# Blockwise attention into a routed MoE on one core: a transpose target moved to another PSUM bank, ten more empty transposes, and the page's index add moved from GpSimd to VectorE

## The chip, the cores and the metric

The kernel is one program on one core of a Trainium2 chip. Its time is the device time of one launch in microseconds (us). Several launches are timed and their median is compared; one further launch is taken with the hardware profiler, and the rows below come from that one.

The five engines run their own instruction lists and meet at semaphores: TensorE (PE, with its weight loads as PEld), VectorE (DVE), ScalarE (ACT), GpSimd (POOL) and SyncE (SP), which here only starts transfers.

## The reference, cut to what matters

```python
# attention: 8 batches x 8 heads, 576 tokens, head width 64, causal in blocks of 64
scores = q @ k.T / 8, masked where block(row) < block(column)
x = softmax(scores) @ v                      # becomes 4608 tokens x 512
# mixture of experts: 8 experts, one per token
expert = argmax(x @ w_gate);  gate = softmax(x @ w_gate)[expert]
for e in range(8):                           # tokens sorted by expert
    y[e's tokens] = relu(x[e's tokens] @ w1[e]) @ w2[e]     # 512 -> 1024 -> 512
out = gate * y, every token's row put back in its place
```

## The kernel before, in words

**Attention.** The 64 heads are taken two at a time, as 32 pairs. For a pair `p`, `load` fetches q and k, `cast` makes fp16 of them in `h16`, and `trans` turns nine 128x128 blocks on TensorE into a PSUM tile, from which VectorE or ScalarE copies them to `qkT`. `scores_0`, `scores_1` and `scores_2` are the matmuls of the scores into the PSUM tiles `sA` and `sB`, each followed by its exponentials on ScalarE into `pt`; `scores_2` also makes two 64-column pieces (`last_64`), one in `o1[:, 384:448]` and one in `f0[:, 0:64]`, whose exponentials go to `p4`. `attend` multiplies by v into `oP` and `o1`, `sums` and `totals` make the softmax's denominators.

All engines run under a manual schedule: the order in which the Python code is called is the order on each engine. The loop over `p` scores pair `p + 1` while pair `p` is attended. Ahead of the loop stands an **opening** that does the first pair and half of the second: 42 empty transposes (`warm`, which turn the identity and whose result nobody reads), the cast and turns of pair 0, eight more empty turns, the cast of pair 1, `scores_0(0)`, `scores_1(0)`, the turns of pair 1, `scores_2(0)`, and twelve more empty turns. The PSUM tiles are banks of 2 KB per partition: `sA` and `sB` take two each, `oP`, `o1`, `f0` and `f1` one each; `oP16`, `o116`, `f016` and `f116` are the same banks read as fp16.

**MoE.** Tokens are scattered into DRAM in order of expert (`xsorted`), and taken back as pages of 128 rows. This draw has 38 pages, T = 0 to 37. `page(T)` issues, in this order: on TensorE `m1(T)` (32 matmuls into `sA` or `sB`), the four turns of `mtx(T + 2)`, and `m2(T - 1)` (8 matmuls into `oP` or `f0`); on VectorE the copy of page `T + 2`'s first weights into a stage (`mstage`, L614) and the copy of its turned rows (L623); on ScalarE the relu of `m1` (L635) and the scaled copy of `m2`'s result into a buffer y (L647). Then GpSimd makes the token index of page `T - 1` in one of four small tiles (`tos`) by adding a void flag to the index that came with the page (L649, L655; a plain copy at L652), and `write_out` starts the indirect DMA that puts y's rows into `out` (L660). From page 14 on GpSimd also starts the indirect DMA that fetches page `T + 6` (`mload`, L595), behind that page's write. After the fetches of pages 26 and 35, GpSimd is drained (L688). The last pages, from 36, stand in nested conditions, since the number of pages is known only on the chip; the very last write takes `y_last` and `to_last`.

Of the kernel before, what the change touches and what calls it, by code (L numbers as in the profile page):

```python
# [12 lines left out]
ALU = mybir.AluOpType  # L13
# [11 lines left out]
def kernel(  # L25
# [10 lines left out]
    nc = tc.nc  # L36
# [31 lines left out]
    oP16, o116, f016, f116 = (t.bitcast(F16) for t in (oP, o1, f0, f1))  # L68
    sA16 = sA.rearrange("p h f -> p (h f)").bitcast(F16)
    sB16 = sB.rearrange("p h f -> p (h f)").bitcast(F16)  # L70
# [37 lines left out]
    def constants():  # L108
        nc.gpsimd.memset(wg, 0.0)
        nc.gpsimd.memset(picks, 0.0)  # L110
        nc.gpsimd.memset(picks[:, 2 * E + 1:2 * E + 2], 1.0)
        for t in oTs:
            nc.gpsimd.memset(t[:, 576:640], 0.0)

        for t in vts:
            nc.gpsimd.memset(t[0:64, 4], 0.0)
# [37 lines left out]
    def unmixed(did, kind, others):  # L154

        tc.declare_no_dep(did.ins, group=others, reason="the first pages are of other experts")
        tc.add_to_no_dep_group(kind, did.ins)
# [44 lines left out]
    def copy(engine, dst, src):  # L202
        if engine is nc.scalar:
            nc.scalar.activation(dst, src, AF.Copy)  # L204
        else:
            engine.tensor_copy(dst, src)  # L206
# [6 lines left out]
    def warm(ps, n):  # L213

        for _ in range(n):
            nc.tensor.transpose(ps[:, 0:128], ident16, ident16)  # L216

    def trans(p, parts):
        for ps, c0, c1, *engines in parts:
            for c in range(c0, c1):  # L220
                nc.tensor.transpose(ps[:, (c - c0) * 128:(c - c0) * 128 + 128], h16[:, c],  # L221
                                    ident16)
        for n in range(2):
            for ps, c0, c1, *engines in parts:
                to = qkTs[p % 2][:, n].rearrange("d (a p c) -> d a p c", c=9, p=32)
                turned = ps[:, 0:(c1 - c0) * 128].rearrange("d (c a n p) -> d n a p c", n=2,
                                                            a=2, p=32)
                copy(engines[n], to[:, :, :, c0:c1], turned[:, n])
# [15 lines left out]
    def scores_1(p):  # L244
        pt = pts[p % 2]
        score(p, 1, sB, 0, 192, 384)
        score(p, 3, sB, 384, 448, 128)
        exp(pt[:, :, 640:1024], sB[:, :, 0:384])
        exp(pt[:, :, 1088:1216], sB[:, :, 384:512])
# [3 lines left out]
    def scores_2(p):  # L253

        pt, qkT = pts[p % 2], qkTs[p % 2]
        for at, c in enumerate((0, 1, 3, 2)):
            score(p, c, sA, at * 64, c * 128, 64)
        score(p, 2, sA, 256, 320, 256)
        for h, ps in enumerate(last_64):
            r = slice(h * 64, h * 64 + 64)  # L260
            nc.tensor.matmul(out=ps, lhsT=qkT[r, 1, 448:576],
                             rhs=qkT[r, 0, 512:576], start=True, stop=True,
                             skip_group_check=True)
        for h, ps in enumerate(last_64):
            exp(p4s[p % 2][:, h], ps)
        for a, b, w, o in ((0, 1152, 576, 0), (1024, 1408, 192, 128)):
            exp(pt[:, :, a:b].rearrange("p h (c x) -> p h c x", x=w)[:, :, :, 0:64],
                sA[:, :, o:o + 128].rearrange("p h (c x) -> p h c x", c=2), bias=maskb)
        exp(pt[:, :, 1280:1536], sA[:, :, 256:512])
# [103 lines left out]
    def choose(b):  # L373

        lg, mx, val, m2 = (tmp(n, w) for n, w in (
            ("lg", (128, 5, E)), ("mx", 5), ("val", (128, 5, E)), ("m2", 5)))
        oh = ohs[b % 2]
        nc.vector.reduce_max(out=mx, in_=lg, axis=AX.X)
        nc.vector.tensor_tensor(out=lg, in0=lg, in1=over_e(mx), op=ALU.subtract)
        nc.vector.scalar_tensor_tensor(out=val, in0=lg, scalar=0.0, in1=pref,  # L380
                                       op0=ALU.is_equal, op1=ALU.mult)
        nc.vector.reduce_max(out=m2, in_=val, axis=AX.X)
        nc.vector.tensor_tensor(out=oh, in0=val, in1=over_e(m2), op=ALU.is_equal)
# [38 lines left out]
    def scatter(b, j):  # L422
# [14 lines left out]
    rest_e, rest_r, void = (vts[2].rearrange("p c h d -> p (c h d)").bitcast(I32)[  # L437
        :, 512 + i * REST:512 + i * REST + REST] for i in range(3))
# [9 lines left out]
    def spare(i, n):  # L448
# [5 lines left out]
    first_e, first_r, early_void = (  # L454
        ends_of.bitcast(I32)[:, 3 * REST + i * FIRST:3 * REST + i * FIRST + n]
        for i, n in enumerate((FIRST, FIRST, EARLY)))
# [180 lines left out]
    def m2(T, last=False):  # L637
        yp, hT, xs = yps[T % 2], hTs[T % 2], xss[T % XS]
        y, to = (y_last, to_last) if last else (ys[T % len(ys)], tos[T % 4])
        for f in range(8):  # L640
            did = nc.tensor.matmul(  # L641
                out=yp, lhsT=hT[:, f * 128:f * 128 + 128],
                rhs=wall[:, ds(pg[ET.PE, T], 1), 8 + f, :].rearrange("p a f -> p (a f)"),
                start=(f == 0), stop=(f == 7))
            if T < EARLY:
                unmixed(did, "early pages", "late weights")
        nc.scalar.activation(y, yp, AF.Copy, scale=xs.bitcast(F32)[:, 256:257])  # L647
        if T < EARLY:
            nc.gpsimd.tensor_tensor(out=to, in0=xs[:, 257:258], in1=early_void[:, T:T + 1],  # L649
                                    op=ALU.add)  # L650
        elif T < FIRST:
            nc.gpsimd.tensor_copy(to, xs[:, 257:258])  # L652
        else:
            t = T - FIRST
            nc.gpsimd.tensor_tensor(out=to, in0=xs[:, 257:258], in1=void[:, t:t + 1], op=ALU.add)  # L655
        if not last:
            write_out(to, y)

    def write_out(to, y):
        did = nc.gpsimd.indirect_dma_start(  # L660
            out=out[:, :], out_offset=bass.IndirectOffsetOnAxis(ap=to, axis=0),
            in_=y, in_offset=None, bounds_check=N - 1, oob_is_err=False)
        apart("out", did)

    def page(T, first_product=True):

        certain, near = N // 128, 3
        if T + near >= certain + XS - 2 and T + near < PAGES:
            mload(T + near)
        if first_product:  # L670
            m1(T)
        steps = [lambda: m2(T - 1)] if T > 0 else []

        for t in (4, 5) if T == 2 else (T + 3,) if T != 1 else ():
            if t < PAGES:
                mexpert(t, ET.PE)
        if T + 2 < PAGES:
            mexpert(T + 2, ET.DVE)
            mstage(T + 2)

            steps.insert(1 if T == 1 else 0, lambda: mtx(T + 2, xps[T % 2]))
        for step in steps:
            step()
        if 1 < T < certain and T - 2 + XS < certain + XS - 2:
            mload(T - 2 + XS)
        if T in (FIRST, certain - 7):

            nc.gpsimd.drain()  # L688
# [14 lines left out]
    with tc.manual_schedule(engines={ET.PE, ET.Activation, ET.DVE, ET.Pool, ET.SP}):  # L703
# [12 lines left out]
        nc.gpsimd.memset(maskb[0:64], 0.0)  # L716
        scores_0(0)
        scores_1(0)
        trans(1, ((f016, 0, 6, nc.vector, nc.vector), (oP16, 6, 9, nc.vector, nc.vector)))
        scores_2(0)  # L720
        warm(sB16, 12)
        constants()
        load(3)
        cast(2)
        for h in range(2):
            nc.sync.dma_start(
                out=wg[h * 64:h * 64 + 64, :, h * E:h * E + E],
# [152 lines left out]
```

## Time and profile before

| | us |
|---|---|
| median of three runs | 367.33 |
| the three runs | 367.33, 364.81, 367.8 |
| the profiled execution, its own time | 367.39 |
| its span, first to last instruction | 365.5 |
| TensorE busy in the span | 348.9 (95%) |
| GpSimd busy in the span | 241.0 (66%) |

The span is the part of the device time that the trace covers; 1.89 us of the profiled execution lie around it. Busy time counts what an engine executes, and a share of the span is an average over stages that differ. The granted clock of TensorE is a share of its full speed: 1.00 is 2.4 GHz, 0.50 is 1.2 GHz.

### The profile page before, as it was taken

How to read it: one execution, taken by the hardware profiler on the slowest of the kernel's cores; microseconds unless marked ns; L12 is line 12 of the kernel's file. 1: busy time of each engine (PE TensorE's matmuls, PEld its weight loads, DVE VectorE, ACT ScalarE, POOL GpSimd, SP SyncE). 2: the span in 40 equal slices, each digit the busy share in tenths (PEclk: the TensorE clock that was granted, in tenths of full speed). 3: DMA queues.
4: the chain of work that ended last, by engine and by line, in shares of the span. 5: the costliest groups of instructions: out<-in, count | busy, mean ns of one | idle time of the engine just before them, and what ended most of it. 6: DMA issues, size and time to landing. Idle time of an engine off the chain costs nothing.

```text
span 365.5 us, 12734 instructions
## 1 busy us (share of the span) xinstructions
PE 348.9 (95%) x4870; PEld 232.3 (64%) x4870; DVE 238.2 (65%) x517; ACT 233.4 (64%) x454; POOL 241.0 (66%) x330
## 2 busy tenths in 40 slices
PE   7899999999999999999999999999999999999970
PEld 6456665666666565656565687777777776777740
DVE  2678788788787878887888985853443435343420
ACT  3688787888887888878888734444444444444430
POOL 2364338658568386587486688788667748885881
PEclk9899999999999999999999999999999999999995
DMA  8889999999989999999960429999523222331221
GB/s 189 198 185 241 240 224 267 247 238 275 242 182 273 259 253 272 228 267 255 239 168 4 131 64 212 242 226 220 165 95 101 99 65 101 102 117 47 97 75 62
DMA packets 70818, 65.47 MB, mean 179 GB/s; under 512 B 43743, under 2 KB 54495, under 8 KB 70752
## 3 DMA queue, kind: packets, MB, share of 16 engines
q0 software_dynamic: 18688, 33.47, 40.8%
q1 hardware_dynamic: 51744, 30.54, 33.5%
q8 instruction: 41, 0.67, 0.8%
q10 hardware_dynamic: 320, 0.59, 0.7%
q14 instruction: 25, 0.20, 0.2%
HBM read 67.73 MB, written 14.97 MB: 226 GB/s over the span
## 4 chain that ended last, share of the span: by engine, by line
PE 87%; DMA 5%; POOL 2%; issue 2%; ACT 1%; POOLq 1%; DVE 1%
PE oP L284 26%; PE f L305 8%; PE sA L629 8%; PE sB L629 7%; PE oP L641 7%; PE f L641 7%; PE sA L234 6%; PE sB L221 5%; PE f L340 4%; DMA out_dram<-v,to 4%; PE sB L234 2%; PE f L216 1%; POOL qk L595 1%; PE o L284 1%; PE o L342 1%
## 5 line engine op out<-in xcount | busy, mean ns | idle before, releaser
L284 PE MATMUL oP<-pt,v 128*64 128x320 f32 (+3 forms) x512 | 98.3, 490 | 0.0
L614 DVE COPY pt<-wall 128x4096 f16 (+1 forms) x40 | 49.6, 1242 | 68.2 <-PE sB L629 34.0
L206 POOL CAST h<-qk 128x1152 f16<-128x1152 f32 (+2 forms) x32 | 36.1, 1128 | 63.2 <-PE sB L221 38.0
L629 PEld LDWEIGHTS <-pt 128*128 128x128 f16 x1216 | 70.8, 98 | 8.2 <-issue 0.2
L238 ACT ACTIVATE pt<-sA 128x1024 f32<-128x1024 f32 x64 | 52.6, 822 | 19.5 <-PE sA L234 19.5
L426 POOL DMA_INDIRECT xsorted<-x,slot x40 | 48.4, 1210 | 13.9 <-POOL slot L425 9.5
L292 DVE TENSOR_TENSOR acc<-acc,pt 128x640 f32<-128x640 f32 x64 | 44.3, 692 | 4.4
L641 PEld LDWEIGHTS <-qkT 128*128 128x128 f16 x304 | 28.2, 98 | 27.4 <-issue 0.2
L660 POOL DMA_INDIRECT out_dram<-v,to x25 | 32.4, 1295 | 13.9 <-issue 4.3
L284 PEld LDWEIGHTS oP<-pt,v 128*64 128x64 f32 x512 | 28.6, 137 | 20.3 <-issue 11.6
L629 PE MATMUL sA<-h,pt 128*128 128x128 f16 x608 | 37.1, 219 | 0.0
L629 PE MATMUL sB<-h,pt 128*128 128x128 f16 x608 | 37.0, 219 | 0.0
L641 PE MATMUL oP<-wall,qkT 128*128 x152 | 35.9, 379 | 0.2 <-issue 0.2
L641 PE MATMUL f<-wall,qkT 128*128 x152 | 35.9, 379 | 0.0
L292 DVE TENSOR_TENSOR acc<-pt 128x896 f32<-128x896 f32 x32 | 35.1, 1098 | 0.6 <-ACT pt L238 0.5
L234 PEld LDWEIGHTS <-qkT 64*128 64x128 f16 x512 | 13.4, 95 | 33.6 <-issue 23.0
L238 ACT ACTIVATE pt<-sB 128x768 f32<-128x768 f32 x64 | 34.5, 596 | 0.0
L635 ACT ACTIVATE qkT<-sA 128x1024 f16<-128x1024 f32 x19 | 19.5, 1024 | 22.7 <-PE sA L629 22.7
L595 POOL DMA_INDIRECT qk<-xsorted,v x22 | 29.5, 1340 | 6.7 <-issue 3.4
L635 ACT ACTIVATE qkT<-sB 128x1024 f16<-128x1024 f32 x19 | 19.5, 1024 | 21.6 <-PE sB L629 21.6
L204 ACT ACTIVATE qkT<-sB 128x576 f16<-128x576 f16 x43 | 27.0, 672 | 1.4
L238 ACT ACTIVATE pt<-sA,maskb 128x256 f32<-128x256 f32 x64 | 27.0, 483 | 0.0
(165 smaller groups left out, 610.8 us busy)
## 6 DMA issues: line engine op xcount, KB each, us to landing
wall<-in_moe_w_dram POOLq DMA_DIRECT2D x32, 512.0 KB, 8.8
qk<-in_q_dram SPq DMA_DIRECT2D x64, 144.0 KB
qk<-in_k_dram SPq DMA_DIRECT2D x60, 144.0 KB
v<-in_v_dram SPq DMA_DIRECT2D x64, 128.0 KB
qk<-xsorted SPq DMA_DIRECT2D x20, 136.0 KB
v<-in_v_dram SPq DMA_DIRECT2D x32, 32.0 KB
xsorted<-x,slot POOLq DMA_INDIRECT x40, 6.4
qk<-in_k_dram ACTq DMA_DIRECT2D x4, 144.0 KB
```

The lines of the kernel that those rows point to most:

```text
L206: engine.tensor_copy(dst, src)
L234: nc.tensor.matmul(out=ps[:, h, o:o + w], lhsT=qkT[r, 1, c * 128:c * 128 + 128], rhs=qkT[r, 0, q0:q0 + w], start=True, stop=True)
L238: nc.scalar.activation(dst, src, AF.Exp, scale=scale, **kw)
L284: nc.tensor.matmul(out=o[h * 64:h * 64 + 64], lhsT=vt[:, c, h, :], rhs=src, start=(c == 0), stop=(c == 4 or to is None), skip_group_check= ...
L292: nc.vector.tensor_tensor(out=acc[:, :, at:], in0=acc[:, :, at:] if at else pt[:, :, 128:576], in1=out if at else pt[:, :, 576:1024], op=A ...
L426: did = nc.gpsimd.indirect_dma_start(out=xsorted[:, :], out_offset=bass.IndirectOffsetOnAxis(ap=slot[0:m, :], axis=0), in_=x16s[b % 2][0:m ...
L595: did = nc.gpsimd.indirect_dma_start(out=xss[T % XS], out_offset=None, in_=xsorted[:, :], in_offset=bass.IndirectOffsetOnAxis(ap=rest_r[:, ...
L614: else engine.tensor_copy(dst, src[:, x])
L629: nc.tensor.matmul(out=hp[:, f // 4, f % 4 * 128:f % 4 * 128 + 128], lhsT=stages[T % 2][:, c // 2, c % 2 * 1024 + f * 128:c % 2 * 1024 + f ...
L635: nc.scalar.activation(hTs[T % 2], hp.rearrange("p a f -> p (a f)"), AF.Relu)
L641: did = nc.tensor.matmul(out=yp, lhsT=hT[:, f * 128:f * 128 + 128], rhs=wall[:, ds(pg[ET.PE, T], 1), 8 + f, :].rearrange("p a f -> p (a f) ...
L660: did = nc.gpsimd.indirect_dma_start(out=out[:, :], out_offset=bass.IndirectOffsetOnAxis(ap=to, axis=0), in_=y, in_offset=None, bounds_che ...
```

## The change

It has three parts. The first six turned blocks of pair 1 go to `o116` in place of `f016`. The empty turns behind `scores_2(0)` are 22 in place of 12 and go to `f116` in place of `sB16`. The three forms of the token index are issued on VectorE in place of GpSimd.

```diff
@@ m2
         if T < EARLY:
-            nc.gpsimd.tensor_tensor(out=to, in0=xs[:, 257:258], in1=early_void[:, T:T + 1],
+            nc.vector.tensor_tensor(out=to, in0=xs[:, 257:258], in1=early_void[:, T:T + 1],
                                     op=ALU.add)
         elif T < FIRST:
-            nc.gpsimd.tensor_copy(to, xs[:, 257:258])
+            nc.vector.tensor_copy(to, xs[:, 257:258])
         else:
             t = T - FIRST
-            nc.gpsimd.tensor_tensor(out=to, in0=xs[:, 257:258], in1=void[:, t:t + 1], op=ALU.add)
+            nc.vector.tensor_tensor(out=to, in0=xs[:, 257:258], in1=void[:, t:t + 1], op=ALU.add)
@@ the opening
-        trans(1, ((f016, 0, 6, nc.vector, nc.vector), (oP16, 6, 9, nc.vector, nc.vector)))
+        trans(1, ((o116, 0, 6, nc.vector, nc.vector), (oP16, 6, 9, nc.vector, nc.vector)))
         scores_2(0)
-        warm(sB16, 12)
+        warm(f116, 22)
```

On TensorE in the opening, before: the end of `scores_2(0)`, the first empty turn into `sB`, and what follows (`o_67` is `o1`, `f_68` is `f0`, `f_69` is `f1`, `qkT_75` belongs to pair 0 and `qkT_76` to pair 1; the words in brackets are the engines whose semaphores the row waits for).

```order
L234 MATMUL sA<-qkT_75 128x256
L261 LDWEIGHTS qkT_75
L261 MATMUL o_67<-qkT_75 128x64
L261 LDWEIGHTS qkT_75
L261 MATMUL f_68<-qkT_75 128x64 [waits DVE_49]
L216 LDWEIGHTS ident_96
L216 MATMUL sB<-ident_96 128x128 [waits Activation_49]
```

The wait for VectorE stands at the second of the two 64-column pieces, the one in `f0`.

The same place on TensorE in the changed kernel.

```order
L234 MATMUL sA<-qkT_75 128x256
L261 LDWEIGHTS qkT_75
L261 MATMUL o_67<-qkT_75 128x64 [waits DVE_49]
L261 LDWEIGHTS qkT_75
L261 MATMUL f_68<-qkT_75 128x64
L216 LDWEIGHTS ident_96
L216 MATMUL f_69<-ident_96 128x128
```

The wait for VectorE stands at the first piece now, the one in `o1`; in both programs it asks for the same count, which VectorE reaches with the third of its four copies of pair 1's turned blocks. The empty turns wait for nothing.

On GpSimd in the late pages, before: a write, a fetch, an index, the next write and fetch.

```order
L660 DMA out_dram<-oT_87,to_116 4608x512 [waits Activation_49,Pool_49]
L595 DMA qk_0_71<-xsorted,v_83 128x272 [waits DMASW2_49,PE_49]
L655 TENSOR_TENSOR to_113<-qk_0_71,v_83 128x1 [waits DMASW3_49]
L660 DMA out_dram<-v_81,to_113 4608x512 [waits Activation_49,Pool_49]
L595 DMA qk_1_72<-xsorted,v_83 128x272 [waits DMASW4_49,PE_49]
```

The same stretch of GpSimd in the changed kernel.

```order
L660 DMA out_dram<-oT_87,to_114 4608x512 [waits DMASW5_49,DVE_49,Activation_49]
L595 DMA qk_0_71<-xsorted,v_83 128x272 [waits DMAHW2_49,DMASW6_49,PE_49]
L660 DMA out_dram<-v_81,to_115 4608x512 [waits DMASW7_49,DVE_49,Activation_49]
L595 DMA qk_1_72<-xsorted,v_83 128x272 [waits DMAHW3_49,DMASW0_49,PE_49]
L660 DMA out_dram<-v_82,to_116 4608x512 [waits DMASW1_49,DVE_49,Activation_49]
```

The index is gone from this list, and each write waits for VectorE and for a transfer (DMASW) itself.

On VectorE in the late pages of the changed kernel, two pages (`pt` is the stage, `h_74` the turned rows).

```order
L614 COPY pt_77<-wall 128x2x2048 [waits DVE_49,PE_49]
L623 COPY h_74<-o_67 128x512 [waits DVE_49,PE_49]
L655 ISA to_114<-qk_2_73,v_83 128x2 [waits DMASW5_49,DMASW0_49]
L605 TENSOR_LOAD v_83
L614 ISA
L614 COPY pt_78<-wall 128x2x2048 [waits DVE_49,PE_49]
L623 COPY h_74<-f_69 128x512 [waits DVE_49,PE_49]
L655 ISA to_115<-qk_0_71,v_83 128x2 [waits DMASW7_49,DMASW2_49]
```

The index stands behind the page's two copies and ahead of the next page's. It is an instruction of another form (ISA, over two halves of the integer), and it waits for two transfers: the fetch of its page, and the write that used the same small tile four pages earlier.

## Rows read from the trace of the kernel before

**Rows 1.** The page's second part: 40 equal slices of the span.

```profile
PE   7899999999999999999999999999999999999970
PEclk9899999999999999999999999999999999999995
```

**Rows 2.** Timeline of TensorE, 8 to 24 us: start, duration, engine, line.

```profile
9.99 0.19 PE L261 MATMUL o<-qkT 64*128 64x64 f16 x1
11.05 0.19 PE L261 MATMUL f<-qkT 64*128 64x64 f16 x1 [0.87 <-DVE qkT L206]
11.17 0.84 PE L216 MATMUL sB<-ident 128*128 128x128 f16 x12
12.77 0.58 PE L234 MATMUL sA<-qkT 64*128 64x512 f16 x2 [0.75 <-ACT pt L238]
...
16.82 0.40 PE L234 MATMUL sA<-qkT 64*128 64x64 f16 x10
...
19.61 0.39 PE L234 MATMUL sA<-qkT 64*128 64x512 f16 x2
...
22.03 0.40 PE L234 MATMUL sA<-qkT 64*128 64x64 f16 x10
```

**Rows 3.** Timeline of all engines in the opening.

```profile
10.27 0.24 ACT L238 ACTIVATE p<-o 128x64 f32<-128x64 f32 x1
...
10.47 0.53 DVE L206 COPY qkT<-f 128x384 f16<-128x384 f16 x1
...
11.28 0.22 ACT L238 ACTIVATE p<-f 128x64 f32<-128x64 f32 x1 [0.76 <-PE f L261]
...
11.40 0.83 ACT L238 ACTIVATE pt<-sA,maskb 128x256 f32<-128x256 f32 x2
```

**Rows 4.** Busy time by stretch: us, each engine's busy time, granted clock, DMA share, GB/s.

```profile
13.00:14.00 1.00, 1.00 (x8) 0.48 (x6) 0.90 (x1) 0.62 (x1) 0.00 (x0) 0.50 1.06 261
...
16.00:17.00 1.00, 1.00 (x14) 0.18 (x12) 0.00 (x0) 0.16 (x1) 0.00 (x0) 0.87 0.83 191
```

**Rows 5.** Timeline of one page, from 320 us.

```profile
320.16 1.23 DVE L614 COPY pt<-wall 128x4096 f16 x1 [2.18 <-PE sB L629]
...
320.38 1.92 POOL L595 DMA_INDIRECT qk<-xsorted,v  x1 [0.30 <-PE sB L629]
321.31 0.42 DVE L623 COPY h<-f 128x512 f16<-128x512 f16 x1
...
322.32 0.20 POOL L655 TENSOR_TENSOR to<-qk,v 128x1 int32<-128x1 int32 x1
322.80 1.00 POOL L660 DMA_INDIRECT out_dram<-v,to  x1 [0.28 <-POOL to L655]
```

**Rows 6.** Timeline from 325 us, across the second drain of GpSimd.

```profile
325.85 0.69 ACT L647 ACTIVATE oT<-f,qk 128x512 f32<-128x512 f32 x1 [0.87 <-PE f L641]
...
333.16 0.99 POOL L660 DMA_INDIRECT out_dram<-oT,to  x1 [0.51 <-POOL to L655]
...
335.53 1.03 POOL L655 TENSOR_TENSOR to<-qk,v 128x1 int32<-128x1 int32 x1
```

**Rows 7.** Timeline from 353 us: the last page's result, and GpSimd's last three writes.

```profile
353.78 0.69 ACT L647 ACTIVATE acc<-f,qk 128x512 f32<-128x512 f32 x1 [1.09 <-PE f L641]
...
354.45 1.00 POOL L660 DMA_INDIRECT out_dram<-oT,to  x1 [0.28 <-POOL to L655]
...
357.45 1.00 POOL L660 DMA_INDIRECT out_dram<-acc,to_last  x1 [0.28 <-POOL to_last L655]
```

**Rows 8.** Timeline at 266 us: the result of page 13, and its write.

```profile
266.06 0.69 ACT L647 ACTIVATE v<-f,qk 128x512 f32<-128x512 f32 x1 [0.87 <-PE f L641]
...
267.52 1.67 POOL L660 DMA_INDIRECT out_dram<-v,to  x1 [1.81 <-issue]
```

**Rows 9.** Timeline at 228 us: a small add of VectorE.

```profile
228.40 0.15 DVE L525 TENSOR_TENSOR cnt<-base,region 128x8 f32<-128x8 f32 x1
```

**Rows 10.** The instructions on the index tiles: from a write's issue to its landing.

```profile
DMA to landing us min/median/max: 2.6/3.4/6.3
```

## The prediction

> **What bounds the kernel now.** I read the slices of the span first. TensorE is busy nine tenths or more from the third slice to the thirty-eighth, and its granted clock is full in all of them but the second and the last [rows 1]. So in between nothing but TensorE's own work counts, and what can be won lies at the two ends: before about 17 us, and after TensorE's last matmul at about 354 us.
>
> The opening, next, in TensorE's timeline [rows 2]. It stands idle twice. The 64-column piece in `f0` waits 0.87 us, until 11.05, for VectorE's copy out of `f0`, which runs from 10.47 to 11.00 [rows 3]; behind the twelve empty turns the scores of pair 1 wait 0.75 us, until 12.77, for ScalarE's exponentials. After the second gap the granted clock is 0.50, which is 1.2 GHz, for all of 13 to 16 us and comes back within the next microsecond [rows 4]. From the first of pair 1's scores to the ten short matmuls of `scores_2(1)` it takes 16.82 - 12.77 = 4.05 us; the same rows one pair later, at 2.4 GHz, take 22.03 - 19.61 = 2.42 us [rows 2]. The low clock costs 1.63 us.
>
> The end, last. The last page's result is ready at 353.78 + 0.69 = 354.47, but its write starts only at 357.45 [rows 7], 2.98 us later. Where GpSimd isn't behind, a write starts 267.52 - (266.06 + 0.69) = 0.77 us after its result [rows 8]. So 2.21 us of the end are GpSimd's arrears. They date from the second drain: page 29's result is ready at 326.54 and its write starts at 333.16, 6.62 us later [rows 6]. GpSimd can hardly work them off, since a page lasts (325.85 - 266.06) / 16 = 3.74 us [rows 6, 8] and GpSimd's own list takes 1.92 + 0.20 + 0.28 + 1.00 + 0.30 = 3.70 us of it [rows 5].
>
> **The turns into `o1`.** In intention this frees the 64-column pieces from the copies. By the order of the changed program it doesn't: the wait for VectorE, for the same count, has only moved from the second piece to the first, so both start at about 11.05. The first piece's exponential, which ran at 10.27 beside other work, now comes behind the wait as well, and the steps on ScalarE there follow each other at 0.12 us (11.28 to 11.40) [rows 3]. So pair 1's scores come 0.12 us later, at 12.89: **+0.12**.
>
> **Ten more empty turns.** Twelve took 0.84 us [rows 2], at most 0.07 each; 22 take at most 1.54 and end by 11.20 + 1.54 = 12.74, ahead of 12.89. They are hidden behind the exponentials; were these 0.2 us shorter, the turns would cost the difference. They also no longer wait for the exponentials of `sB`, which were done anyway. What they bring is less idleness ahead of the stretch at 1.2 GHz: of the two gaps, 0.87 and 0.75 us, the second shrinks to 0.15 to 0.4 us. The trace has no stretch with just that idleness, so the value has two ends: nothing, if the clock falls all the same, and the whole 1.63 us. In the first slice TensorE is busy seven tenths only and the clock stays full [rows 1], and with the second gap closed the stretch ahead of 12.8 us is about as full as that, so I take **-1.63**, and keep the other end as a rival. The work behind the opening follows at once, since TensorE sets the pace there.
>
> The Trainium skill, "TensorE: Matmul & The Clock Gate", section "What's actually happening", says that the clock follows the engine's recent activity and that the judging doesn't start anew with the kernel, so that the change of level falls elsewhere in each run. No row here shows two runs' clocks. By that rule some runs of the kernel before keep the clock, the 364.81 run perhaps, and for these the turns would be worth nothing: +0.12 in place of -1.51.
>
> **The index on VectorE.** There are 38 of them. On VectorE each is an instruction whose form no row shows; the nearest are VectorE's small add, 0.15 us [rows 9], and GpSimd's own, 0.20 to 1.03 us [rows 5, 6]. I take 0.2, since the work is VectorE's. It stands behind the page's two copies, where VectorE then idles 2.18 us [rows 5], so up to that length it costs nothing. It adds a wait for the write that used the same tile four pages earlier. Behind it in the queue stands the next page's stage copy, for which TensorE waits two pages on. The add would run at 321.31 + 0.42 = 321.73, 1.07 us before that page's write is due at 322.80 [rows 5]; four pages are 14.96 us, so the earlier write has 13.9 us from its own due time. Its worst is 6.62 us of arrears, 1.67 us of issue and 6.3 us to land [rows 6, 8, 10], 14.6 us: 0.7 us late, still inside the 2.18 us.
>
> On GpSimd each page loses the add; what this wins shows only where GpSimd is last, at the end. The low bound: the last three writes start 354.45 and 357.45, 1.50 us apart, and each loses an add of 0.20 [rows 5, 7], 0.60 in all. The high bound is the whole of the arrears, 2.21. In between: after the drain the add takes 1.03 us [rows 6], because it meets VectorE's copy, and with the add gone the next transfer's issue meets the copy in its place, as the fetch of 1.92 us does [rows 5]; so not all comes back. On the other side GpSimd reaches the drain earlier. I take **-1.5**, a little above the middle. The transfers that SyncE and ScalarE start are not touched.
>
> **The sum.** The profiled execution took 367.39 us, 0.06 above the median of the runs shown. 367.39 + 0.12 - 1.63 - 1.5 = **364.4 us**, 0.8% less. The forecast's own range, by the tail's bounds, is 363.7 to 365.3. A difference under 1%, 3.7 us, can't be told from none here, with runs from 364.81 to 367.8.
>
> **Rivals.** *The clock falls again.* The 0.87 us gap stays, and the stretch ahead of it has pauses of its own; then 367.39 + 0.12 - 1.5 = 366.0. Against it stands only that the second gap is nearly closed.
>
> *GpSimd's freed time is taken by VectorE's copies*, page after page, because each page's fetch or write is held up until the copy ends (1.92 us against about 1.0) [rows 5]; the tail then gains the 0.60 alone: 367.39 - 1.51 - 0.6 = 365.3. The Trainium skill, "SBUF — State Buffer", section "Who interferes with whom", says that a VectorE instruction with two inputs in SBUF, as the moved add is, holds off a GpSimd instruction that reads SBUF; that would work the same way.
>
> *More comes back.* GpSimd works off all arrears before the second drain and again behind it: 367.39 - 1.51 - 2.21 = 363.7; if the new median lies where the lowest run lies now, 364.81 + 0.12 - 2.21 = 362.7. For it speaks that GpSimd's list of a page drops from 3.70 to 3.50 us against TensorE's 3.74, and further where a fetch misses the copy.
>
> *The add is dear on VectorE*, the case that ends slower. It is one mechanism: an add longer than the 2.18 us of idle pushes every later stage copy, and TensorE waits for the excess in each of some 37 pages. At 2.4 us that is 37 x 0.22 = 8 us, 372 us or more. Below 2.18 us it is nothing. The rows of small adds speak against it, the unseen form for it.
>
> *The wait at `o1` is passed early after all*, against the order: then up to 0.87 us more, 363.5.
>
> **Chances.** Forecast 0.46, clock falls 0.18, freed time taken 0.10, more comes back 0.20, dear add 0.05, early pass 0.01. Faster by over 1% means under 363.66: the fourth and the last, and a little of the forecast's lower edge, 0.26. Slower by over 1%: 0.05. Within 1%: 0.69. The range goes from 362.7 to the clock's rival with a tail of 1.0, 366.5; it leaves out the dear add and little else.
>
> **What would show it.** In the changed kernel's opening: the piece in `o1` at about 11.05 behind a wait for VectorE, 22 turns ending by 12.7, pair 1's scores at 12.9, and a granted clock of 1.00 from 12 to 17 us, the ten short matmuls coming 2.4 us behind the scores. In the pages: VectorE's add near 0.2 us behind the two copies with the stage copies 3.74 us apart as before. At the end: the last write 0.8 to 2.4 us behind the last result, in place of 2.98. A clock of 0.50 anywhere behind the turns, an add beyond 2 us or a late last write would each refute its step. The whole would be wrong if some other wait fills TensorE's stretch between the ends, which the rows of before can't show.

## The result, and the profile after

The changed kernel takes 361.18 us (median of four runs, 360.77 to 362.13), the kernel before 367.04 beside it (364.81 to 367.8): a ratio of 0.9854, 95% interval 0.9806 to 0.9901. It is faster by about twice what was forecast, and lies below the range.

| | before | after |
|---|---|---|
| the profiled execution, its own time | 367.39 | 360.77 |
| its span | 365.5 | 358.7 |
| last page's result is ready | 354.47 | 352.90 |
| last write starts | 357.45 | 353.18 |
| GpSimd's last branch | 360.6 | 356.0 |
| GpSimd's final drain starts | 363.3 | 356.5 |

So the 6.8 us between the spans fall into three pieces: 1.57 up to the last result, 4.27 - 1.57 = 2.70 from there to the last write, and 8.05 - 5.52 = 2.53 from the last write to the end of the span.

The page's slices of the changed kernel, which answer to [rows 1]: the low clock of the second slice is gone.

```profile
PE   6899999999999999999999999999999999999992
PEclk9999999999999999999999999999999999999999
```

The opening, in the timeline of the changed kernel (TensorE and ScalarE), answers to [rows 2, 3]:

```profile
11.02 0.19 PE L261 MATMUL o<-qkT 64*128 64x64 f16 x1 [0.89 <-DVE qkT L206]
11.03 0.20 PE L261 MATMUL f<-qkT 64*128 64x64 f16 x1
11.16 1.40 PE L216 MATMUL f<-ident 128*128 128x128 f16 x22
12.85 0.39 PE L234 MATMUL sA<-qkT 64*128 64x512 f16 x2 [0.29 <-ACT pt L238]
...
15.27 0.40 PE L234 MATMUL sA<-qkT 64*128 64x64 f16 x10
...
11.25 0.22 ACT L238 ACTIVATE p<-o 128x64 f32<-128x64 f32 x1 [0.64 <-PE f L261]
```

The wait for VectorE's copy stands ahead of the first 64-column piece now and is as long as before, 0.89 us against 0.87. The scores of pair 1 start at 12.85, 0.08 later than before; the second gap has shrunk from 0.75 to 0.29; and the ten short matmuls follow 2.42 us behind the scores in place of 4.05. The stretches of [rows 4] are at full clock (the third figure from the right):

```profile
13.00:14.00 1.00, 1.00 (x10) 0.44 (x8) 1.00 (x1) 0.72 (x1) 0.06 (x1) 1.00 0.88 232
16.00:17.00 1.00, 1.00 (x14) 0.63 (x13) 0.59 (x1) 1.00 (x4) 0.57 (x1) 1.00 0.90 240
```

VectorE's index add, by form (its count, then us in all and mean ns of one), stands against the 0.15 us of [rows 9]. Below it is the time from the start of a write to its landing, 5.2 us in the median where [rows 10] have 3.4:

```profile
L655 DVE CUSTOM_DVE_ANT_0 to<-qk,v 128x2 uint16<-128x2 uint16 x17 | 2.5, 147 | 0.0
...
L652 DVE COPY to<-qk 128x1 int32<-128x1 int32 x8 | 1.1, 143 | 0.0
```

```profile
DMA to landing us min/median/max: 4.5/5.2/5.9
```

The end, in the timeline of the changed kernel (GpSimd and ScalarE), answers to [rows 6 to 8]:

```profile
327.99 0.99 POOL L660 DMA_INDIRECT out_dram<-oT,to  x1 [3.52 <-DVE to L655]
...
343.93 0.99 POOL L660 DMA_INDIRECT out_dram<-oT,to  x1 [0.64 <-ACT oT L647]
...
352.21 0.69 ACT L647 ACTIVATE acc<-f,qk 128x512 f32<-128x512 f32 x1 [1.09 <-PE f L641]
...
353.18 0.97 POOL L660 DMA_INDIRECT out_dram<-acc,to_last  x1 [0.80 <-ACT acc L647]
```

The gap of 3.52 us ahead of 327.99 is that of the second drain. After it GpSimd works its arrears off: from 343.93 on it is GpSimd that waits for ScalarE's result. The last write starts 353.18 - 352.90 = 0.28 us after its result. That is less than the 0.77 of a write with no arrears before [rows 8].

Behind the last write, by source line: GpSimd's conditional branches, whose last start is the second time, and its drains at the program's end, whose first start is the first time. Before:

```profile
L696 POOLq COMPARE_BRANCH  x4: 37/42/58, 352.0 to 360.6; - x4
...
L875 POOLq DRAIN  x3: 52/103/1362, 363.3 to 365.2; - x3
```

and after:

```profile
L696 POOLq COMPARE_BRANCH  x4: 38/42/50, 344.3 to 356.0; - x4
...
L875 POOLq DRAIN  x3: 52/103/1362, 356.5 to 358.4; - x3
```

The branch out of the nested conditions jumps over the code of the pages that this input doesn't have, to the final drain. It takes 2.7 us before and 0.5 after. In the gap of the kernel before stands one packet of a queue that the page calls `instruction`, at 361.6 us; the changed kernel has none in its gap. The remaining 0.3 us of this piece is the wait for the last write, 3.15 us from its start to the branch before and 2.82 after. In the profiles below this wait goes from 2.1 to 4.1 us with no order in it, so the 0.3 isn't counted as an effect of the change.

### The profile page after: what moved, and what is told of

It is laid out like the page before. It is cut to its first block, busy times and chain, and to the rows that moved or that the text cites. A ratio compares the mean times of both kernels' runs of the same rounds, so it can differ in the third digit from the quotient of the medians.

```text
span 358.7 us, 12780 instructions
## 1 busy us (share of the span) xinstructions
PE 347.6 (97%) x4880; PEld 232.4 (65%) x4880; DVE 240.3 (67%) x555; ACT 233.1 (65%) x454; POOL 224.7 (63%) x292
## 4 chain that ended last, share of the span: by engine, by line
PE 91%; DMA 6%; ACT 0%; ACTq 0%; POOL 0%; DVE 0%; issue 0%; POOLq 0%
PE oP L284 26%; PE sA L629 9%; PE f L305 9%; PE sB L629 8%; PE oP L641 8%; PE f L641 8%; PE sA L234 6%; PE sB L221 5%; DMA out_dram<-v,to 5%; PE f L340 4%; PE sB L234 2%; DMA qk<-in_k_dram 2%; PE o L621 1%; PE f L621 1%; PE o L284 1%; PE o L342 1%
## 5 line engine op out<-in xcount | busy, mean ns | idle before, releaser
L284 PE MATMUL oP<-pt,v 128*64 128x320 f32 (+3 forms) x512 | 97.0, 485 | 0.0
L629 PEld LDWEIGHTS <-pt 128*128 128x128 f16 x1216 | 70.8, 98 | 8.2 <-issue 0.2
L426 POOL DMA_INDIRECT xsorted<-x,slot x40 | 49.4, 1235 | 14.0 <-POOL slot L425 11.0
L660 POOL DMA_INDIRECT out_dram<-v,to x25 | 28.5, 1141 | 24.6 <-ACT v L647 19.5
L629 PE MATMUL sA<-h,pt 128*128 128x128 f16 x608 | 37.1, 219 | 0.0
L629 PE MATMUL sB<-h,pt 128*128 128x128 f16 x608 | 37.0, 219 | 0.0
L595 POOL DMA_INDIRECT qk<-xsorted,v x22 | 32.2, 1466 | 6.7 <-issue 3.1
L635 ACT ACTIVATE qkT<-sA 128x1024 f16<-128x1024 f32 x19 | 19.4, 1023 | 22.6 <-PE sA L629 22.6
L635 ACT ACTIVATE qkT<-sB 128x1024 f16<-128x1024 f32 x19 | 19.5, 1024 | 21.6 <-PE sB L629 21.6
```

Of the source, the lines that this page charges most:

```text
L284: nc.tensor.matmul(out=o[h * 64:h * 64 + 64], lhsT=vt[:, c, h, :], rhs=src, start=(c == 0), stop=(c == 4 or to is None), skip_group_check= ...
L426: did = nc.gpsimd.indirect_dma_start(out=xsorted[:, :], out_offset=bass.IndirectOffsetOnAxis(ap=slot[0:m, :], axis=0), in_=x16s[b % 2][0:m ...
L595: did = nc.gpsimd.indirect_dma_start(out=xss[T % XS], out_offset=None, in_=xsorted[:, :], in_offset=bass.IndirectOffsetOnAxis(ap=rest_r[:, ...
L629: nc.tensor.matmul(out=hp[:, f // 4, f % 4 * 128:f % 4 * 128 + 128], lhsT=stages[T % 2][:, c // 2, c % 2 * 1024 + f * 128:c % 2 * 1024 + f ...
L635: nc.scalar.activation(hTs[T % 2], hp.rearrange("p a f -> p (a f)"), AF.Relu)
```

## The experiments

E1 to E4 ran on one chip, and so did E5 to E8, E9 to E12, E13 and E14, and E15 and E16, each time beside the kernel before. The chip of E1 to E4 is slower for every kernel (before: 373.01 us), as is that of E15 and E16 (375.28, one run); on the others before takes 365.87 to 366.61, and the ratios are what is compared. A ratio, which stands with its 95% interval, can differ by up to 0.0025 from the quotient of the two medians. "Exit" is the time from GpSimd's last branch to its final drain.

Two theories stood after the first reading. *The ends*: the gain is the sum of what the two profiles show, 1.6 for the clock, 2.7 at the last write, 2.5 at the exit, and the pages are untouched. *Chance and code*: the clock's part belongs to the one profiled run, or the exit's part to GpSimd's shorter list of instructions and not to the writes.

**E1, the two edits in the opening alone.**

```diff
 whole change, but the three index forms:
-            nc.vector.tensor_tensor(out=to, ...
+            nc.gpsimd.tensor_tensor(out=to, ...
```

> The kernel before with the turns into o1 and the 22 empty turns, the index left on GpSimd. Theory: the opening is worth about 1.6 us (granted clock 1.00 from 12 to 17 us, pair 1's scores to the short matmuls 2.4 us) and nothing else moves: the last write still starts about 3 us behind the last result and the program still ends about 8 us behind the last write's start; 365.4 us. Rival: the early end of the opening also lets GpSimd come out of its arrears: then the last write starts within 1 us of the last result, about 362.5 us.

0.9969 (0.9936 to 1.0003). The clock fell in this profile too, with the 22 empty turns, only earlier than in [rows 4] and just as they begin:

```profile
11.00:13.00 2.00, 1.86 (x19) 1.82 (x19) 1.33 (x3) 1.56 (x5) 0.89 (x1) 0.57 1.23 224
13.00:17.00 4.00, 4.00 (x39) 1.71 (x38) 2.62 (x4) 2.12 (x4) 1.20 (x1) 0.79 0.73 182
```

At the low clock the 22 turns are not hidden: they take 2.53 us in place of 1.40, and the scores of pair 1 follow them without a wait, 0.89 us later than in the whole change.

```profile
11.28 2.53 PE L216 MATMUL f<-ident 128*128 128x128 f16 x22
13.74 0.61 PE L234 MATMUL sA<-qkT 64*128 64x512 f16 x2
```

GpSimd has no arrears at the end here: it is done with the write before at 362.45. (TensorE's pages last 0.6 us longer in all than before; whether that is the reason isn't shown.) So its timeline shows the floor with the index on GpSimd. The last result is ready at 362.47:

```profile
362.47 0.20 POOL L655 TENSOR_TENSOR to_last<-qk,v 128x1 int32<-128x1 int32 x1
363.25 1.00 POOL L660 DMA_INDIRECT out_dram<-acc,to_last  x1 [0.57 <-POOL to_last L655]
```

0.78 us, as in [rows 8], against 0.27 in E2 and E4 on the same chip. So half a microsecond of the last write's gain needs no arrears.

**E2, the index on VectorE alone** (the opening as before).

```diff
 kernel before, all three index forms:
-            nc.gpsimd.tensor_tensor(out=to, ...
+            nc.vector.tensor_tensor(out=to, ...
```

> The kernel before with the index on VectorE and nothing else. Theory: this is the larger part of the change, 5.2 us in two pieces: the last write starts about 0.3 us behind the last result in place of 2.98 (2.7 us), and the program ends about 5.5 us behind the last write's start in place of 8.05 (2.5 us); 361.9 us, with the opening's 1.6 us at the low clock still in it. Rival: the second piece is no effect of the index but of that one run; then 364.4 us with an end of 8 us behind the last write's start.

1.0033 (1.0004 to 1.0061): no gain on this chip, though the exit is short (0.4 us) and the last write starts 0.27 us behind its result. The 38 relus of the pages (L635) spread over 142.1 us here, over 138.9 in E1 and 138.4 before. TensorE pauses within a page, in the midst of 32 matmuls, for no wait that its timeline shows:

```profile
312.03 0.44 PE L629 MATMUL sB<-h,pt 128*128 128x128 f16 x5 [0.23 <-issue]
312.75 0.23 PE L629 MATMUL sB<-h,pt 128*128 128x128 f16 x1 [0.28 <-issue]
313.45 1.24 PE L629 MATMUL sB<-h,pt 128*128 128x128 f16 x19 [0.47 <-issue]
```

**E3, the whole change with a small GpSimd memset in every page from 35 on**, so that GpSimd's list is nearly as long as before.

```diff
+        if T >= N // 128 - 1:
+            nc.gpsimd.memset(spacer, 0.0)
```

> The changed kernel with a one-element memset on GpSimd ahead of each write from page 35 on, in the nested conditions too, which puts an instruction back where the index stood without making anything wait for it. Theory (the end is shorter because the code between the last branch and the program's end is shorter, so that GpSimd has it at hand): from the last write's start to the end it takes 8 us again, about 363.5 us, and GpSimd's drain stands more than 2 us behind its last branch. Rival (the length of the code in the conditions does not matter): 5.5 us again, 361.2 us.

1.0061 (1.0028 to 1.0094), with the pages 141.9 us long, as in E2. The exit is long again, 2.6 us, though the last write is as early as after the change:

```profile
L699 POOLq COMPARE_BRANCH  x4: 38/42/58, 358.1 to 370.4; - x4
...
L878 POOLq DRAIN  x3: 52/103/1362, 373.0 to 374.9; - x3
```

**E4, the whole change with twelve empty turns.**

```diff
-        warm(f116, 22)
+        warm(f116, 12)
```

> The changed kernel with 12 empty turns in place of 22. Theory (the ten further turns keep the clock up): granted clock 0.50 for some 3 us from about 13 us, and 1.6 us more, 362.8 us. Rival (the clock fell in the kernel before for another reason, or by chance of that run): granted clock 1.00, 361.2 us.

1.0027 (0.9998 to 1.0055). The clock was low from 13 to 16 us, the exit took 0.5 us, the pages 142.2. Its median is 1.2 us below that of E3, which has the 22 turns, and its exit is 2.1 us shorter; the 0.9 us between would be what the turns are worth, and the two intervals are wider than that.

**E5, the whole change again; E6, E1 again; E7, E2 again; E8, the turns of pair 1 back in `f0`**, all on another chip.

```diff
 E8
-        trans(1, ((o116, 0, 6, nc.vector, nc.vector), ...
+        trans(1, ((f016, 0, 6, nc.vector, nc.vector), ...
```

> The changed kernel as it stands, beside the parts of it on the same chip. If its gain is the sum of what its first profile showed at the two ends (opening 1.55, last write 2.70, exit 2.53 us, the pages 3.74 us as before), it is 6 to 7 us below the kernel before on any chip, a ratio of 0.981 to 0.985. Rival: on a chip where TensorE pauses in the pages for no wait that the profile shows, the index on VectorE costs some 3.5 us there (the stage copies of the pages took 3.2 us longer in E2, E3 and E4 than in E1); then it is 0.99 to 1.00 there, and the stage copies show gaps of 5 to 7 us with a short one behind each.

0.9851 (0.981 to 0.9892): the result again, 361.06 against 366.38. In its profile one wait in the attention cost 1.6 us that the first profile of the change doesn't have (waits of TensorE: total, times, longest). That run's own time is 362.36, the longest of the four.

```profile
PE f L305 <- DVE lgp L332: 1.6, 1, 1.6
```

> The two edits in the opening alone (the index stays on GpSimd). By the ends: 1.5 us less than before, 0.996, last write 0.6 to 3 us behind the last result, 2.6 us from GpSimd's last branch to its final drain. Rival (more of the change's gain comes from the clock than one profile shows): 0.990 or less.

1.0011 (0.9985 to 1.0037): no gain, though the profile is at full clock throughout the opening. Its last write starts 2.97 us behind the result and the exit takes 2.6, both as before.

> The index on VectorE alone (the opening as before). By the ends: 4.7 to 5.2 us less than before, 0.986 to 0.987, last write 0.3 us behind the last result, 0.5 us from GpSimd's last branch to its final drain, TensorE's clock low for 3 us in the opening. By the pages' rival on a chip with TensorE's pauses: 1.00, as E2 was.

0.9882 (0.9835 to 0.993): nearly the whole gain, with last write 0.27 behind its result and exit 0.5. And with twelve empty turns and both gaps of [rows 2], 0.86 and 0.75 us, the clock stayed up:

```profile
11.00:13.00 2.00, 1.25 (x17) 0.95 (x18) 1.45 (x2) 1.44 (x4) 1.14 (x1) 1.00 1.22 244
13.00:17.00 4.00, 4.00 (x47) 2.05 (x45) 3.28 (x5) 3.51 (x9) 0.71 (x1) 1.00 0.64 159
```

> Changed kernel with the second pair's turns back in f0 (22 empty turns and VectorE's index stay). If the other bank does nothing, since the wait for VectorE's copy has only moved from the second 64-column piece to the first: within 0.3 us of the whole change beside it, the clock full from 10 to 17 us. If the bank is what keeps the clock up: 1.5 us more, a granted clock of 0.50 for some 3 us around 13 to 16.

0.9874 (0.9835 to 0.9912), with the wait of 0.88 us ahead of the other piece and the clock full. The other bank brings nothing that can be measured.

**E9, the kernel before with the index on VectorE only in pages that this input never reaches; E10, the reverse.** What runs is unchanged in both; only the list gets shorter or longer.

```diff
 E9, from the kernel before
-            nc.gpsimd.tensor_tensor(out=to, in0=xs[:, 257:258], in1=void[:, t:t + 1], op=ALU.add)
+            add = nc.vector if T >= 39 else nc.gpsimd
+            add.tensor_tensor(out=to, in0=xs[:, 257:258], in1=void[:, t:t + 1], op=ALU.add)
 E10, from the whole change: nc.gpsimd if T >= 39 else nc.vector
```

> The kernel before, with the index on VectorE only in the pages that this input never reaches (39 and later). Nothing that runs is changed; the code that GpSimd jumps over behind its last branch falls from 275 instructions to 230 (229 in the whole change). If the exit's gain is that jump, GpSimd's final drain comes 0.4 to 0.5 us behind its last branch in place of 2.6, with no fetch of instructions between, and the kernel is about 2.2 us (0.6%) faster than before, 0.994; the last write still starts 2.2 to 3 us behind the last result. Rival (the exit is short because GpSimd comes to it in another state, with its writes caught up): 2.6 us as before and 1.000.

0.9997 (0.9974 to 1.002). The jump got nearly as short as in the whole change, and yet the exit took 2.6 us:

```profile
L697 POOLq COMPARE_BRANCH  x4: 38/42/58, 351.8 to 361.3; - x4
...
L876 POOLq DRAIN  x3: 52/103/1362, 363.9 to 365.8; - x3
```

> The changed kernel, with the index back on GpSimd only in the pages that this input never reaches. What runs is the whole change; GpSimd's jump is over 274 instructions, as before. By the jump: 2.6 us from the last branch to the final drain, last write still 0.3 us behind the last result; 2.2 us more than the whole change, which ran at 0.985, so 0.991 of before. By the rival: 0.5 us and 0.985.

0.9924 (0.9894 to 0.9955), 362.95 us. The exit takes 2.8 us with everything else as in the whole change, so it is code that never runs that costs 0.7% here:

```profile
L697 POOLq COMPARE_BRANCH  x4: 38/42/58, 344.6 to 355.6; - x4
...
L876 POOLq DRAIN  x3: 52/103/1362, 358.4 to 360.3; - x3
```

Together they put the rival of E9 aside (with its writes caught up, E10 still has the long exit) and leave the length of the jump in doubt.

**E11, the kernel before without GpSimd's second drain.**

```diff
-        if T in (FIRST, certain - 7):
+        if T == FIRST:
```

> The kernel before without GpSimd's second drain, the index still on GpSimd. If its arrears date from that drain and the add alone doesn't keep it back, the last write starts 0.8 us behind the last result (2.98 before), 2.2 us less than before, 0.994, with the exit's 2.6 us still there. If GpSimd falls behind by the add itself, in every page where it meets VectorE's copy: 2 to 3 us behind as before, and no gain.

1.0003 (0.9972 to 1.0035). The last write starts 1.22 us behind its result in place of 2.98, so the drain is where most of the arrears come from. But the longest of the drains at the end now takes 2.84 us in place of 1.36, and most of the 1.76 us is given back there:

```profile
L696 POOLq COMPARE_BRANCH  x4: 38/42/58, 348.5 to 357.1; - x4
...
L875 POOLq DRAIN  x3: 52/103/2837, 359.9 to 363.2; - x3
```

**E12, the whole change with pair 1's turns in banks that nobody reads then.**

```diff
-        trans(1, ((o116, 0, 6, nc.vector, nc.vector), (oP16, 6, 9, nc.vector, nc.vector)))
+        trans(1, ((f116[:, 320:960], 0, 5, nc.vector, nc.vector), (oP16, 5, 9, nc.vector, nc.vector)))
-        warm(f116, 22)
+        warm(sB16, 18)
```

> The changed kernel with the second pair's turns into two banks that nothing reads at that time (five into the second half of f0's neighbour tile, four into oP's), and the empty turns into sB, so that both 64-column pieces wait for no copy. If the wait for VectorE in the opening is on the path: the idle 0.9 us ahead of the first piece is gone and the scores of pair 1 start up to 0.8 us earlier, 359.8 to 360.4 us where the whole change takes 361.1, 0.983 of before. If the exponentials of ScalarE set the time of those scores anyway: they start where they do now, 0.985.

0.9871 (0.9833 to 0.9909), 361.24 us: no better than the whole change. In TensorE's timeline the first wait is gone and the scores of pair 1 start 0.74 earlier:

```profile
10.29 0.19 PE L261 MATMUL o<-qkT 64*128 64x64 f16 x1
...
12.11 0.39 PE L234 MATMUL sA<-qkT 64*128 64x512 f16 x2 [0.39 <-ACT pt L238]
```

A wait of 0.7 us at L305 in the attention, the place of E5's 1.6, took most of that back in this profile, and its pages begin 0.5 us later than in the whole change (first relu at 210.7 and 210.2). Whether it does so in every run, the times can't tell.

**E13, E14: the jump moved without making it longer.** 99 small GpSimd memsets in the attention move the whole change's last branch by 90 instructions (E13); 88 of them move E9's final drain to exactly 128 instructions behind its place in the whole change, and its branch to 125 behind (E14). The expectations of E9, E13 and E14 count the jump from one condition too far on. From the branch that is taken, after page 37, the compiled list has 322 instructions to the final drain in the whole change, 325 in E9 and E14, 368 in E10 and 370 before; so E14's branch stands three instructions short of the place, and not one.

```diff
+            for _ in range(3):
+                nc.gpsimd.memset(spacer, 0.0)
 E14, from E9: range(3 if p % 3 else 2)
```

> The changed kernel with 90 tiny GpSimd memsets during the attention, far ahead of the pages, where GpSimd idles. The jump behind the last branch is over 229 instructions, as in the whole change, but branch and target lie 90 instructions (5760 bytes at 64 each) further on in GpSimd's list. If the place of branch and target in the blocks of 8192 bytes that the instruction queue fetches decides the exit: 2.6 us from the last branch to the final drain, 0.991 of before. If the length of the jump decides (229 short, 230 long would then be a coincidence with something else): 0.5 us and 0.985.

The exit takes 2.8 us. So the length of the jump isn't what decides, since this one is as long as in the whole change. The time, 0.999 (0.9958 to 1.0021), can't be read for the exit alone: the memsets make the attention longer too (the first relu of the pages is at 213.3 us, 210.2 in the whole change).

```profile
L697 POOLq COMPARE_BRANCH  x4: 37/42/58, 347.5 to 359.2; - x4
...
L878 POOLq DRAIN  x3: 52/103/1362, 362.0 to 363.9; - x3
```

> E9 (index of the unreached pages on VectorE, 230 instructions jumped over, 2.6 us) with 79 tiny GpSimd memsets during the attention, which puts the last branch one instruction short of a whole block of 128 instructions behind its place in the changed kernel. By the place in the blocks: 0.5 us from the last branch to the final drain, 2.2 us less than before, 0.994, though the index runs on GpSimd and the last write still starts some 3 us behind the last result. By the length of the jump, or by the arrears of GpSimd: 2.6 us and 1.000.

1.0008 (0.9978 to 1.0038), exit 1.8 us: between the two theories. A packet of the instruction queue still stands in the gap, but 0.1 us behind the branch; in the kernel before it is 1.0 behind.

```profile
L698 POOLq COMPARE_BRANCH  x4: 38/42/50, 351.5 to 359.3; - x4
...
L879 POOLq DRAIN  x3: 52/103/1362, 361.1 to 363.1; - x3
```

**E15, E16: the whole change's list moved by exactly 128 and 256 instructions**, by 137 and 265 such memsets.

```diff
+            for _ in range(128 // 32 + 9 * (p == 5) if p < 32 else 0):
+                nc.gpsimd.memset(spacer, 0.0)
 E16: 256 // 32
```

> The changed kernel with small GpSimd memsets during the attention, so many that the last branch and its target lie exactly 128 instructions (8192 bytes at 64 each) further on than in the whole change. If the place within the fetched blocks of 8192 bytes decides the exit: 0.5 us from the last branch to the final drain, as in the whole change. If the length of GpSimd's list or the place in it as such decides: 2 to 2.8 us, as in E9, E10, E13 and E14.

```profile
L697 POOLq COMPARE_BRANCH  x4: 38/42/50, 352.9 to 364.8; - x4
...
L878 POOLq DRAIN  x3: 52/103/1362, 365.3 to 367.2; - x3
```

> The same by 256 instructions (16384 bytes). By the place in blocks of 8192 or of 16384 bytes: 0.5 us. By the length of the list or the place in it as such: 2 to 2.8 us. If only this one of the two has 0.5 us, the blocks that count are of 16384 bytes.

```profile
L697 POOLq COMPARE_BRANCH  x4: 38/42/50, 360.4 to 372.3; - x4
...
L878 POOLq DRAIN  x3: 52/103/1362, 372.7 to 374.6; - x3
```

0.5 and 0.4 us, with E15's list as long as the longest and E16's longer than all of those that took 1.8 us or more. So the length of the list doesn't decide either, and a move by 128 or 256 changes nothing where one by 90 does: as far as two moves can show, what counts is the place in the list up to a multiple of 128. How far from this place the short exit holds stays open; E14, with the target in that place and the branch three instructions short of it, has 1.8 us. One run each, 369.49 and 376.91 us beside 375.28; E16's clock was low in the opening, with 22 empty turns.

The start of the last packet of that queue puts all nineteen profiles in order, E14 with them. In the nine with a long exit it starts behind the branch, by 1.0 us (in E14 by 0.1), and the drain starts 1.6 to 1.8 us behind the packet. In the ten with a short exit no packet starts between branch and drain; the last one started 1.4 to 3.3 us ahead of the branch. So the long exit looks like a wait for code that is fetched too late; what makes the fetch early or late, beyond the place in the list, isn't shown.

**E17, the whole change a third time.**

> The whole change once more. On a chip like that of E5 (before near 366.5): 0.985. On one like that of E1 to E4 (before at 373 or more, TensorE pausing in the pages for no wait that the profile shows): if the index on VectorE lengthens the pages there by some 3 us, as E2 to E4 against E1 say, about 0.995 to 1.00; if those four differed by the opening and by chance alone, 0.985.

It came to a chip on which before takes 365.87: 361.28 us, 0.9863 (0.981 to 0.9915), as in E5. The question that it was meant for stays open.

## Why the prediction was wrong

**The step that failed is the end of the sum.** The forecast took 1.5 us, and at most 2.21, for everything behind the last result; the profile shows 2.70 + 2.53 there. Two things went wrong.

*The floor.* "The high bound is the whole of the arrears, 2.21" held the 0.77 us of [rows 8] for fixed. It goes with GpSimd's index: with the add on GpSimd a caught-up write starts 0.78 behind its result (E1), with the add on VectorE 0.27 to 0.28 (after, E2, E4, E5, E7). In the two programs, ScalarE's result was waited for by a semaphore instruction ahead of the write, while the write itself waited for GpSimd's add; after the change the write itself waits for ScalarE. For page 13 of the kernel before, that semaphore instruction ends at 266.79, with the result at 266.75, and GpSimd's next instruction starts at 267.30. That the half microsecond comes from this place of the wait is read from the programs and this gap, and no run changes it alone. The arrears themselves went entirely, as the rival "more comes back" had it; the value between the bounds was too timid. GpSimd's list of a page lost the add, 0.20 to 1.03 us [rows 5, 6], and that was enough for it to catch up by 343.93.

*The exit* had no term. The sum stopped at the last write and took what follows as equal. It is 2.2 us in the two profiles: 2.6 to 2.8 from branch to drain in before, E1, E3, E6, E9, E10, E11 and E13, 0.4 to 0.5 in after, E2, E4, E5, E7, E8, E12, E17 and, moved by 128 and 256 instructions, E15 and E16. E10 gives its price in time: 0.9924 against the 0.9851 of E5 and the 0.9863 of E17, 0.6 to 0.7%, 2.2 to 2.7 us (1.7 by the medians of E10 and E17, which had the same chip; the interval of E10 overlaps that of E17 and not that of E5). No rival had it, and [rows 7] end at the last write: the chain was followed to GpSimd's work and not to the end of the span.

**The clock's term, 1.63, was right for that one profile and too large for the median.** Profile against profile it is 4.05 - 2.42 = 1.63 on the dot. But the level of the clock in the opening is a matter of the run. With twelve empty turns it was low in three of seven profiles (before, E2, E4) and full in four (E7, E9, E11, E14); with 22 it was low in two of eleven (E1, E16). At 1.6 us that makes about (3/7 - 2/11) x 1.6 = 0.4 us for the median, from few profiles. The times allow it: E1 against before -1.0, E6 against before +0.3, E5 against E7 -0.5, with intervals of 1 us and more. The mean granted clock of a run, which stands with every run, doesn't rise with the turns in E6 (0.987 over ten runs, 0.988 over before's nineteen) and does in E1 (0.993 against 0.989), so the ten turns aren't clearly shown to help at all. The prediction named the reason and didn't use it: the Trainium skill, "TensorE: Matmul & The Clock Gate", section "What's actually happening", has the clock follow the engine's recent activity without starting anew at each kernel, so that a level falls at another place in each run. E1 and [rows 4] have it low at 11 to 14.7 and at 13 to 16 us, and E7 not at all.

What the prediction took for a sign that the clock would hold was misread, too. It has the clock full in the first slice, with TensorE busy seven tenths [rows 1]. But the trace of before holds no record of the clock ahead of 6.0 us, and the page's row shows 9 there all the same. TensorE's timeline has the 42 empty turns of that slice at 0.108 us each:

```profile
1.72 4.55 PE L216 MATMUL f<-ident 128*128 128x128 f16 x42 [1.72 <-POOL ident L104]
```

Such turns took 0.064 us each in the changed kernel at a granted clock of 1.00 and 0.115 in E1 at 0.50, so most of that slice's work ran at the pace of the low level. That the term came out to the digit in the first profile was luck.

**Right**: the wait moves to the piece in `o1` and keeps its length (0.89 at 11.02), the turns end before the exponentials do where the clock is full (1.40 us, gap 0.29; not in E1), E8 and E12 put the bank's own worth at nothing measurable; VectorE's add is short (0.15 for the assumed 0.2) and costs no page anything here, with the relus 138.4 us apart from first to last in both kernels. The rival of the dear add fell with that; so did that of GpSimd's freed time, since the last write would have kept its lag. A slip in the chances: the 363.7 of "more comes back" isn't under 363.66, so only its lower case belongs to the 0.26.

The corrected sum for the median is 0.4 + 2.7 + 2.2 = 5.3 us. The measured differences of the medians are 5.86 here, 5.32 in E5, 4.59 in E17, and 4.8 in E7 for the index alone.

**Open.** On the chip of E1 to E4 the index on VectorE brought nothing (E2 to E4, 1.003 to 1.006). There TensorE's pages took 3 us longer with it than in E1, by pauses that no wait explains; E1 has such pauses as well, but fewer (idle time without a wait ahead of L629's weight loads: 0.8 us in E1, 3.5 in E2). On the chip of E15 and E16, just as slow, the pages took 140.9 and 140.3 us. The whole change itself has not been timed on such a chip, so whether it gains there isn't known, nor is the cause of the pauses.

## What to carry to other kernels

Follow the profile to its last line: what stands behind the last write (a branch, a fetch of code, drains) is as much on the path as the write, and an edit that only changes the number of instructions on an engine can shift it, here by 2.2 us. Before counting a clock dip of one profile as a gain, look at whether other runs have it; a median gets only its share. A row that shows the clock full proves nothing where the trace has no record of the clock; how long the instructions took tells it. A floor that is read from the trace, as a write's 0.77 us behind its result, belongs to the waits as they stand, and a change that moves a wait can lower it.

## What the runs showed of the hardware that had not been expected

- GpSimd's jump out of nested conditions took 0.4 to 0.5 us or 2.6 to 2.8 us, by where branch and target lie in its list: a move by 90 instructions made it long (E13), moves by 128 and 256 left it short (E15, E16). Of two jumps over 322 and 325 instructions one took 0.5 and the other 2.6 us; in one place it took 1.8 (E14). In every long exit a packet of the instruction queue starts behind the branch, and the drain 1.6 to 1.8 us behind the packet; the page of before counts 25 packets and 0.20 MB for this queue, so 8 KB each.
- Leaving out GpSimd's second drain moved part of its cost to the end: the longest of the final drains grew from 1.36 to 2.84 us (E11).
- VectorE does the 32-bit integer add as an instruction of its own form on 128x2 16-bit halves, in 0.15 us.
